# Talking-heads attention feeding a rational feed-forward layer: q padded to 128 columns, x, k and v moved in spaced pieces with a second v buffer, and the first tile's scores spread over three pairs of banks and two queues

## The chip, the cores and the metric

One core of a Trainium2 chip. A core has TensorE (PE, with its weight loads shown apart as PEld), VectorE (DVE), ScalarE (ACT), GpSimd (POOL) and SyncE (SP), which here does nothing but issue DMAs. The metric is the device time of one execution in microseconds, as the median of several runs; lower is better.

## The reference

Shapes: batch 4, 12 heads, 448 rows, head dimension 64; the feed-forward layer goes from 768 to 2048 and back over 1792 tokens.

```python
scores = scale * np.matmul(q, k.transpose(0, 1, 3, 2))
scores = np.einsum('bhij,hg->bgij', scores, w_pre)       # heads mixed before the softmax
attn = np.exp(scores - scores.max(-1, keepdims=True))
attn = attn / (attn.sum(-1, keepdims=True) + 1e-09)
attn = np.einsum('bhij,hg->bgij', attn, w_post)          # and after it
x = np.matmul(attn, v)                                   # -> (1792, 768)
h = x @ w_in
P = a0 + a1*h + a2*h**2 + a3*h**3
Q = 1 + abs(b0)*abs(h) + abs(b1)*h**2
out = (P / (Q + 1e-06)) @ w_out
```

## The kernel before, in words

The attention half works in 16 tiles T of query rows, four to a batch b: three of 120 rows and a short one of 88 (T = 0, 7, 11 and 15), held as 9 blocks of 10 rows. For each pair of heads `put_qk` (L428) multiplies q by k: one head in the lower 64 partitions, the other in the upper, each in two pieces of columns, `for i0, i1 in ((0, 64), (64, n))` (L435), with n = 120 or 90. The two results stand in two PSUM banks, taken from the pool `ps_s` of two. DVE or ACT copies each to a tile `st`, and SP issues a DMA, the shuffle (d<-st, L452), that lays the rows of ten blocks and twelve heads beside each other as D, so that one matmul can mix the heads. D has two buffers; a tile of twelve heads needs 13 shuffles, as the last head takes two.

`put_pre` (L488) takes two row blocks at a time, a step: it mixes the heads (PE, L504), takes the row maximum (DVE, L511), the exponential (ACT, L520) and the scale of each row. A tile has six steps, a short one five. The first step of a tile waits for all 13 shuffles of the tile. `put_post` (L562) mixes the heads again two steps later (PE, L569), and `put_av` (L607) multiplies by v twice for each tile (L618), two and three steps into the tile that follows. ACT casts that result into `xs` (L627), which holds x of one batch in one buffer; DVE writes the remainder (L631), and when the last tile of a batch is done, SP stores xs in two halves (L634), each of 1344 KB. v has one buffer and is loaded in four parts (L597), k two buffers (b > 0 in two parts, L351), q three (L339). Beside all this 36 of the 64 pieces of the feed-forward weights are loaded (cr, L367), turned from 64-bit into a pair of numbers by ACT, POOL and DVE, and stored (w_scr, L406); the other 28 follow in the second half.

The second half has 64 units. Each multiplies x by a part of w_in (PE, L762), goes through the rational function on ACT and DVE (its reciprocal, L796, is the longest), and multiplies by w_out (L836).

The order of every engine's work is set by a planner (`Plan.run`): each operation is added with engine, duration, dependencies, a due time `at` and sometimes an earliest time `since`. The planner walks through time on its own durations, takes for each free engine the ready operation with the earliest due time, and the program is written out in that order. Due times come from `tau`, which counts SLOT microseconds a step. The engines then run that order with semaphores, so a DMA that waits on SP holds back every DMA behind it.

Of the kernel before, what the change touches and what calls it, by code (L numbers as in the profile page):

```python
# [235 lines left out]
def mixed_attention_then_rational_ffn(ctx: ExitStack, tc, q, k, v, w, wmix, mask, a, b2, out):  # L236
# [25 lines left out]
    open_pools(base, "left", (("cr", 3), ("cm", 2), ("cg", 1), ("co", 2), ("xs", 1), ("xo", 2)))  # L262
    open_pools(left, "left", (("d", 1), ("e", 6), ("a", 2), ("v", 1)))
# [20 lines left out]
    SLOT, HALF = 4.4, 2.5  # L284
# [51 lines left out]
    def put_q(T, at):  # L336
        def load():
            Q[T] = sb["q"].tile([128, H // 2, TI], F32, tag="q", name="q")
            nc.sync.dma_start(out=Q[T], in_=q[T])  # L339

        q_ld[T] = add("sp", 0.63, load, [R["q"].take()], at=at, extra=dma(128 * H // 2 * TI * 4))

    def put_k(b, parts, at):
# [11 lines left out]
        for i in range(parts):  # L355
            k_ld[b].append(add("sp", 0.63, load(i), [free] + k_ld[b][:1], at=at + 0.8 * i, extra=dma(128 * n * S * 4)))
# [4 lines left out]
    def put_w(f, c, at):  # L361
# [57 lines left out]
        o8 = add("sp", 0.45, store, [o7], at=at, extra=dma(128 * CV * 8))  # L419
# [8 lines left out]
    def put_qk(T, pr, at):  # L428
# [17 lines left out]

        def shuffle(h, i0, i1):
            def fn():
# [3 lines left out]
                nc.sync.dma_start(  # L452
# [3 lines left out]
        slots = [R["ps_s"].take(), R["ps_s"].take()]  # L456
        o = pe(0.82, mm, [q_ld[T], k_ld[b][pr * len(k_ld[b]) // (H // 2)]] + slots, at=at, extra=0.16, mode="quarters")
        qk_op[T, pr] = o
        for hh in range(2):
# [4 lines left out]
            for i0, i1 in ((0, G10),) if h < H - 1 else ((0, G10 - 1), (G10 - 1, G10)):
# [5 lines left out]
                s_ = add("sp", 0.79, shuffle(h, i0, i1), [x for x in deps if x], at=at, extra=0.06 * (i1 - i0) * n / TI, after=after)  # L470
# [121 lines left out]
    def put_v(b, at):  # L592
# [14 lines left out]
    def put_av(T, hv, at):  # L607
# [365 lines left out]
```

## Time and profile before

| what | value |
|---|---|
| median of 3 runs | 1002.48 us (997.08 to 1003.05) |
| the profiled execution | 1004.43 us |
| its span | 1002.7 us |
| mean granted TensorE clock | 0.967 |
| busy share: PE, DVE, ACT, POOL | 92%, 78%, 46%, 28% |
| DMA | 173.58 MB, mean 173 GB/s |
| first step of tile 0 / first unit of the second half | 27.18 us / 523.02 us |

The span runs from the first to the last instruction of the profiled execution. PEclk is the share of TensorE's full clock, 2.4 GHz, that was granted. A row such as `[11.25 <-DMA d<-st]` says that the engine stood idle for 11.25 us before it and that the landing of a shuffle ended the wait. DMA share is the mean busy share of the core's 16 DMA engines.

### The profile page before, as it was taken

To read this page: it belongs to the slowest core of one execution; us is meant where nothing else is said; L and a number is where in the kernel's file an instruction comes from. 1 tells how busy PE (TensorE), PEld (TensorE's weight loads), DVE (VectorE), ACT (ScalarE), POOL (GpSimd) and SP (SyncE) were. 2 spreads that over 40 slices of the span, in tenths; PEclk is the share of its full clock that TensorE was granted. 3 is DMA by queue.
4 is the path that set the end of the run, shared out by engine and by line. 5 is a ranking of instruction groups with operands and counts; after the bars stand their busy time and mean duration, and the time that the engine had idled before them with its cause. 6 is when DMAs were issued, how large, how long until landed. Compare 5 with 4: busy or idle time off the path is not lost.

```text
span 1002.7 us, 17820 instructions
## 1 busy us (share of the span) xinstructions
PE 923.0 (92%) x6768; PEld 726.3 (72%) x6768; DVE 784.7 (78%) x1198; ACT 461.9 (46%) x1066; POOL 281.1 (28%) x288
## 2 busy tenths in 40 slices
PE   5878998699996999789989999999999999999996
PEld 1345666456564656555678999889899999999995
DVE  3657777587685886656758899999998889898995
ACT  2456566356564656534545355555533323333230
POOL 2222332233323333200242454555211111111110
PEclk9789999799998999989989999999999999999999
DMA  6864757655676556832569474643456141330212
GB/s 209 231 196 149 241 171 249 216 176 183 197 258 216 168 167 189 273 116 90 216 220 417 187 255 126 221 166 111 150 196 248 52 163 58 147 111 1 72 39 74
DMA packets 67561, 173.58 MB, mean 173 GB/s; under 512 B 6452, under 2 KB 47508, under 8 KB 63764
## 3 DMA queue, kind: packets, MB, share of 16 engines
q1 hardware_dynamic: 67476, 172.45, 51.3%
q8 instruction: 53, 0.87, 0.4%
q14 instruction: 32, 0.26, 0.1%
HBM read 86.53 MB, written 47.19 MB: 133 GB/s over the span
## 4 chain that ended last, share of the span: by engine, by line
PE 59%; DVE 17%; DMA 12%; issue 4%; ACT 4%; SPq 2%; POOL 2%; POOLq 0%; ACTq 0%; DVEq 0%
PE ps_s L762 15%; PE ps_a L569 10%; PE ps_t L836 7%; PE ps_s L438 7%; PE ps_t L504 6%; DVE rc L796 6%; PE ps_v L618 6%; DMA d<-st 5%; PE ps_a L836 5%; DMA cr<-in_w 4%; PE ps_v L836 2%; DVE cg L386 2%; DVE sq L793 1%; DVE cm L392 1%; SPq L452 1%
## 5 line engine op out<-in xcount | busy, mean ns | idle before, releaser
L569 PEld LDWEIGHTS ps_a<-krs,e 128*112 128x112 f32 x1440 | 157.2, 180 | 68.9 <-DVE nm L511 19.4
L796 DVE RECIPROCAL rc<-sq 128x448 f32<-128x448 f32 x64 | 188.4, 2943 | 0.9
L569 PE MATMUL ps_a<-krs,e 128*112 128x120 f32 x1440 | 174.4, 275 | 0.0
L809 POOL TENSOR_TENSOR g<-rc,g 128x448 fp32r<-128x448 f32 x60 | 71.7, 1195 | 297.4 <-DVE g L232 203.2
L504 PE MATMUL ps_t<-d,kpre 64*64 64x448 f32 x720 | 102.8, 588 | 51.0 <-DMA d<-st 35.1
L438 PE MATMUL ps_s<-kk,q 64*64 64x448 f32 (+2 forms) x768 | 132.9, 584 | 13.6 <-DMA kk<-in_k 6.2
L836 PE MATMUL ps_t<-g,w 128*128 128x448 f32 x576 | 142.6, 366 | 2.3 <-ACT o L875 1.4
L520 ACT ACTIVATE e<-ps_t,nm 128x448 f32<-128x448 f32 x180 | 112.5, 630 | 65.3 <-DVE nm L511 54.2
L511 DVE TENSOR_REDUCE nm<-ps_t 128x1 f32<-128x448 f32 x180 | 104.8, 615 | 48.2 <-PE ps_t L504 47.4
L773 ACT ACTIVATE m<-ps_s,a_sb 128x448 f32<-128x448 f32 x64 | 46.3, 724 | 191.3 <-PE ps_s L762 191.2
L377 POOL TENSOR_SCALAR cm<-cm 128x384 f32<-128x384 f32 x64 | 99.6, 1560 | 84.8 <-ACT cm L372 84.6
L762 PE MATMUL ps_s<-xs,w 128*128 128x448 f32 x576 | 122.4, 366 | 0.6 <-DVE m L789 0.6
L762 PE MATMUL ps_s<-x,w 128*128 128x448 f32 x576 | 121.8, 365 | 0.0
L836 PEld LDWEIGHTS ps_t<-g,w 128*128 128x128 f32 x576 | 107.9, 188 | 12.1 <-ACT o L875 2.2
L762 PEld LDWEIGHTS ps_s<-xs,w 128*128 128x128 f32 x576 | 108.4, 189 | 9.9 <-DVE m L789 1.4
L762 PEld LDWEIGHTS ps_s<-x,w 128*128 128x128 f32 x576 | 108.2, 188 | 8.3
L527 POOL TENSOR_SCALAR sm<-sm 128x2 f32<-128x2 f32 (+1 forms) x92 | 35.9, 390 | 249.1 <-ACT e L520 246.8
L232 DVE COPY aa<-ps_a 112x480 f32<-112x480 f32 x137 | 87.9, 653 | 22.3 <-PE ps_a L569 21.0
L836 PE MATMUL ps_a<-g,w 128*128 128x448 f32 x384 | 98.2, 365 | 0.0
L438 PEld LDWEIGHTS ps_s<-kk,q 64*64 64x64 f32 (+2 forms) x768 | 37.5, 133 | 82.6 <-issue 54.6
L232 DVE COPY st<-ps_s 120x448 f32<-120x448 f32 (+1 forms) x123 | 73.5, 616 | 25.2 <-PE ps_s L438 25.0
L403 POOL TENSOR_TENSOR co<-cm,co 128x384 fp32r<-128x384 f32 x64 | 69.3, 1083 | 76.5 <-ACT co L230 76.3
(47 smaller groups left out, 1104.9 us busy)
## 6 DMA issues: line engine op xcount, KB each, us to landing
d<-st SPq DMA_DIRECT2D x132, 210.0 KB
cr<-in_w SPq DMA_DIRECT2D x64, 384.0 KB
w_scr<-co SPq DMA_DIRECT2D x64, 384.0 KB
w<-w_scr SPq DMA_DIRECT2D x16, 1536.0 KB
x_scr<-xs SPq DMA_DIRECT2D x8, 1344.0 KB
x<-x_scr SPq DMA_DIRECT2D x3, 2688.0 KB
d<-st SPq DMA_DIRECT2D x44, 157.5 KB
q<-in_q SPq DMA_DIRECT2D x16, 360.0 KB
```

The source lines that it names most:

```text
L232: eng.tensor_copy(o, i)
L377: nc.gpsimd.tensor_scalar(out=m, in0=m, scalar1=F64_MIN, scalar2=F64_MAX, op0=ALU.max, op1=ALU.min)
L403: eng.tensor_sub(t[:, 1, :], box["m"].bitcast(F32), t[:, 0, :].bitcast(F32))
L438: nc.tensor.matmul(box["s"][hh][i0:i1, 0:S], lhsT=Q[T][d, pr, i0:i1], rhs=K[b][d, pr, :], start=True, stop=True)
L504: nc.tensor.matmul(box[r if nt == 2 else 0]["t"][64 * c:64 * c + 64, 0:S], lhsT=kpre[p], rhs=Dt[T][p, kb + c if nt == 2 else kb, :], start ...
L511: nc.vector.tensor_reduce(out=nm, in_=box[r]["t"][:, 0:S], axis=AX.X, op=ALU.max, negate=True)
L520: nc.scalar.activation(e, box[r]["t"][:, 0:S], AF.Exp, bias=box[r]["nm"], accum_out=box[0]["sm"][:, r:r + 1])
L569: nc.tensor.matmul(t[0:JT, j * P:(j + 1) * P], lhsT=box["e"][:, j * JT:(j + 1) * JT], rhs=box["kr"], start=True, stop=True)
L762: nc.tensor.matmul(h[:, 0:S], lhsT=W[fi][:, wi, kk * 128:(kk + 1) * 128], rhs=x[:, kk // 3, xj, kk % 3, :], start=(n == 0), stop=(n == 3 * ...
L796: nc.vector.reciprocal(new("rc"), box["vv"])
L809: eng.tensor_sub(g[:, 1, :], box["rc"], g[:, 0, :].bitcast(F32))
L836: nc.tensor.matmul(O[key][:, 0:S], lhsT=W[fi][:, wi, DM + m * 128:DM + (m + 1) * 128], rhs=box["g"][:, gi, :], start=(f == 0 and n == 0), ...
```

## The change

- q is padded from 120 to 128 columns, and the second piece of every pair of heads covers columns 64 to 128. The rows past n are not copied on.
- x of a batch is stored in 12 pieces of 224 KB instead of 2 of 1344 KB, the pieces 1.6 us apart in the plan, the first 5 us after the last value product.
- k of batches 1 to 3 is loaded in 6 pieces 7 us apart instead of 2 that are 0.8 us apart, from 40 us earlier. v has a second buffer, and its four parts are 8 us apart. To make room the output buffers `xo` open only in the second half.
- Tile 0's scores take their two banks in turn from `ps_s`, `ps_t` and `ps_a`, which are idle then, and the shuffles of its odd heads are issued by ACT instead of SP.
- In the plan, stores of w and x count as ready 2 us later than their data (`late`), their issue is costed a little differently, and SLOT is 4.2 instead of 4.4.

```diff
-            t = max([t, op.since] + [d.start for d in op.behind])
+            t = max([t + op.late, op.since] + [d.start for d in op.behind])
...
-    open_pools(base, "left", (("cr", 3), ("cm", 2), ("cg", 1), ("co", 2), ("xs", 1), ("xo", 2)))
-    open_pools(left, "left", (("d", 1), ("e", 6), ("a", 2), ("v", 1)))
+    open_pools(base, "left", (("cr", 3), ("cm", 2), ("cg", 1), ("co", 2), ("xs", 1)))
+    open_pools(left, "left", (("d", 1), ("e", 6), ("a", 2), ("v", 2)))
...
-    SLOT, HALF = 4.4, 2.5
+    SLOT, HALF = 4.2, 2.5
...
-            Q[T] = sb["q"].tile([128, H // 2, TI], F32, tag="q", name="q")
+            Q[T] = sb["q"].tile([128, H // 2, TQ], F32, tag="q", name="q")
...
-            k_ld[b].append(add("sp", 0.63, load(i), [free] + k_ld[b][:1], at=at + 0.8 * i, extra=dma(128 * n * S * 4)))
+            k_ld[b].append(add("sp", 0.45, load(i), [free] + k_ld[b][:1], at=at + gap * i, extra=dma(128 * n * S * 4), since=at + gap * i - 4.0))
...
-        o8 = add("sp", 0.45, store, [o7], at=at, extra=dma(128 * CV * 8))
+        o8 = add("sp", 0.57, store, [o7], at=at, extra=dma(128 * CV * 8), late=2.0)
...
-            box["s"] = [bank("s"), bank("s")]
-            for i0, i1 in ((0, 64), (64, n)):
+            box["s"] = [bank(ps_), bank(ps_)]
+            for i0, i1 in ((0, 64), (64, TQ)):
...
+        def other(h):
+            return T == 0 and h % 2 == 1
...
-                nc.sync.dma_start(
+                (nc.scalar if other(h) else nc.sync).dma_start(
...
-            v_ld[b].append(add("sp", 0.63, load(j), [free] + v_ld[b][:1], at=at, extra=dma(JT * H * D * 4), since=at))
+            v_ld[b].append(add("sp", 0.63, load(j), [free] + v_ld[b][:1], at=at + 8.0 * j, extra=dma(JT * H * D * 4), since=at + 8.0 * j))
...
-        def store():
-            nc.sync.dma_start(out=x_scr[b][:, hv], in_=Xs[b][:, hv].bitcast(F32))
+        def store(hl, p):
+            def fn():
+                nc.sync.dma_start(out=x_scr[b][:, hv, hl, p], in_=Xs[b][:, hv, hl, p].bitcast(F32))
+            return fn
...
-            o = add("sp", 0.63, store, x_done[b, hv], at=at, extra=dma(128 * 6 * S * 4))
+            for i in range(6):
+                o = add("sp", 0.45, store(i // 3, i % 3), x_done[b, hv], at=at + 5.0 + 1.6 * (2 * i + hv),
+                        extra=dma(128 * S * 4), late=2.0, since=at + 4.0 + 1.6 * (2 * i + hv))
...
-        put_k(b, 2, at=tau[first[4 * b - 2]])
+        put_k(b, 6, at=tau[first[4 * b - 2]] - 40.0, gap=7.0)
...
-        put_v(b, at=tau[first[4 * b] + LAG + 2] - 6.0 if b else 10.0)
+        put_v(b, at=tau[first[4 * b]] - 24.0 if b else 10.0)
...
-        put_qk(0, pr, at=-8.0 + pr)
+        put_qk(0, pr, at=-8.0 + pr, ps_="sta"[pr % 3])
```

TensorE's matmuls stand in the same order before and after, with other shapes and, for tile 0, other banks. What the planner moves is on SP and in which of ACT and DVE does a copy.

SP's queue before, in the step of tile 4 in which batch 0's x is done, up to tile 5's last head (x_scr0 is the store of batch 0, vv the load of batch 1's v, d_114 the D that tile 5 will read):

```order
L634 DMA x_scr0_137<-xs_692 128x2688
L452 DMA d_114<-st_1823 10x12x448
L452 DMA d_114<-st_1830 10x12x448
L406 DMA w_scr2_123<-co_1805 256x1x384
L597 DMA vv_1889<-in_v 112x768
L367 DMA cr_1900<-in_w 128x768
L634 DMA x_scr0_137<-xs_692 128x2688
L597 DMA vv_1889<-in_v 112x768 x3
L452 DMA d_114<-st_1907 10x12x448
L452 DMA d_114<-st_1919 9x12x448
```

After, around the same shuffles of tile 5 (d_111 is the same D):

```order
L457 DMA d_111<-st_1827 10x12x448
L457 DMA d_111<-st_1840 10x12x448
L640 DMA x_scr0_134<-xs_686 128x448 x2
L408 DMA w_scr2_120<-co_1817 256x1x384
L640 DMA x_scr0_134<-xs_686 128x448
L353 DMA kk_1647<-in_k 128x448
L369 DMA cr_1897<-in_w 128x768
L341 DMA q_1914<-in_q 128x768
L457 DMA d_111<-st_1916 10x12x448
L457 DMA d_111<-st_1923 9x12x448
```

The two whole stores and the four loads of v have left this place; three pieces of x, one of k and tile 7's q stand there now.

SP's queue before, three steps into the shuffles of tile 6 (d_113), with nothing of batch 0's x left:

```order
L452 DMA d_113<-st_2034 10x12x448
L367 DMA cr_2059<-in_w 128x768
L452 DMA d_113<-st_2070 10x12x448
L452 DMA d_113<-st_2084 10x12x448
L452 DMA d_113<-st_2131 10x12x448
L452 DMA d_113<-st_2135 10x12x448
```

After, at the same shuffles (d_110):

```order
L457 DMA d_110<-st_2034 10x12x448
L640 DMA x_scr0_134<-xs_686 128x448 x3
L353 DMA kk_1647<-in_k 128x448
L457 DMA d_110<-st_2073 10x12x448
L457 DMA d_110<-st_2083 10x12x448
L369 DMA cr_2106<-in_w 128x768
L640 DMA x_scr0_134<-xs_686 128x448
L369 DMA cr_2135<-in_w 128x768
L457 DMA d_110<-st_2139 10x12x448
L457 DMA d_110<-st_2137 10x12x448
```

The last four pieces of x of batch 0 now stand before and behind tile 6's shuffles of its third pair of heads. An ACT cast into the one xs buffer, later in tile 5, waits for them.

TensorE's first rows before, two pairs of heads of tile 0 and the first rows of the third (26 is the second piece of 90 rows):

```order
L438 MATMUL ps_s_162<-kk_151,q_149 64x448
L438 MATMUL ps_s_163<-kk_151,q_149 64x448
L438 MATMUL ps_s_162<-kk_151,q_149 26x448
L438 MATMUL ps_s_163<-kk_151,q_149 26x448
L438 MATMUL ps_s_176<-kk_151,q_149 64x448
L438 MATMUL ps_s_177<-kk_151,q_149 64x448
L438 MATMUL ps_s_176<-kk_151,q_149 26x448
L438 MATMUL ps_s_177<-kk_151,q_149 26x448
L438 MATMUL ps_s_192<-kk_151,q_149 64x448
L438 MATMUL ps_s_193<-kk_151,q_149 64x448
```

After:

```order
L440 MATMUL ps_s_159<-kk_148,q_146 64x448
L440 MATMUL ps_s_160<-kk_148,q_146 64x448
L440 MATMUL ps_s_159<-kk_148,q_146 64x448
L440 MATMUL ps_s_160<-kk_148,q_146 64x448
L440 MATMUL ps_t_166<-kk_148,q_146 64x448
L440 MATMUL ps_t_167<-kk_148,q_146 64x448
L440 MATMUL ps_t_166<-kk_148,q_146 64x448
L440 MATMUL ps_t_167<-kk_148,q_146 64x448
L440 MATMUL ps_a_189<-kk_148,q_146 64x448
...
L440 MATMUL ps_s_195<-kk_148,q_146 64x448
L440 MATMUL ps_s_196<-kk_148,q_146 64x448
```

The second pair takes two banks of ps_t and the third two of ps_a, and the fourth is the first to come back to ps_s; every piece has 64 columns.

ACT's first rows before:

```order
L230 COPY st_172<-ps_s_163 90x448
L331 ACTIVATE b1_sb_119<-b_sb_118 128x1
L230 COPY st_188<-ps_s_177 90x448
L230 COPY st_201<-ps_s_193 90x448
L230 COPY st_213<-ps_s_205 90x448
```

After:

```order
L232 COPY st_175<-ps_s_160 90x448
L457 DMA d_110<-st_175 10x9x448
L333 ACTIVATE b1_sb_116<-b_sb_115 128x1
L457 DMA d_110<-st_184 10x9x448
L232 COPY st_203<-ps_a_190 90x448
L457 DMA d_110<-st_203 10x9x448
L232 COPY st_225<-ps_t_205 90x448
```

ACT now copies and issues in turn; the rows with DMA are the shuffles of tile 0's odd heads.

## Rows read from the trace of the kernel before

**Rows 1.** The windows view: start and end of a stretch in us, its length, then busy time and number of instructions of PE, PEld, DVE, ACT and POOL, the granted clock, DMA share and GB/s. The stretches that begin at 27.18, 146.18, 184.15, 273.56, 308.81, 369.40 and 393.76 us are the whole tiles 0, 4, 5, 8, 9, 11 and 12, from the first step of the tile to that of the next; the last two are the start and the rest of the second half.

```profile
27.18:56.59 29.41, 20.55 (x132) 10.03 (x133) 16.21 (x35) 13.53 (x36) 8.47 (x10) 0.79 0.88 243
146.18:184.15 37.97, 26.72 (x289) 18.77 (x289) 24.44 (x52) 18.57 (x51) 10.62 (x14) 0.89 0.74 243
170.00:180.00 10.00, 2.90 (x27) 1.85 (x19) 5.49 (x14) 3.42 (x9) 2.91 (x4) 0.79 0.96 324
184.00:190.00 6.00, 5.85 (x31) 3.76 (x32) 2.31 (x4) 1.90 (x5) 0.23 (x1) 0.55 0.55 205
184.15:214.97 30.82, 30.01 (x289) 20.16 (x289) 24.02 (x49) 16.38 (x44) 9.96 (x11) 0.91 0.57 184
273.56:308.81 35.25, 26.45 (x282) 16.78 (x281) 24.64 (x56) 17.31 (x48) 9.61 (x13) 0.95 0.77 251
308.81:337.54 28.73, 28.73 (x288) 19.04 (x288) 22.44 (x44) 17.40 (x47) 10.59 (x11) 0.94 0.61 194
369.40:393.76 24.36, 24.07 (x261) 16.53 (x261) 14.73 (x34) 15.20 (x39) 7.50 (x9) 1.00 0.71 222
393.76:430.16 36.40, 25.91 (x282) 16.78 (x281) 24.35 (x56) 17.40 (x48) 8.08 (x12) 0.93 0.72 234
523.02:541.07 18.05, 17.40 (x81) 15.48 (x82) 13.77 (x17) 9.35 (x17) 3.04 (x4) 0.97 1.00 401
541.07:1002.60 461.53, 451.30 (x2224) 417.19 (x2222) 413.53 (x443) 183.66 (x333) 129.98 (x103) 1.00 0.39 138
```

**Rows 2.** The chain that ended last, in order of time, around tiles 5, 6, 9, 11 and 13: start us, length us, what. x8 and x16 are one step's pre-mix, one pair of heads' scores, one step's post-mix; x48 is one of a tile's two value products.

```profile
190.30 0.91 PE ps_t L504 x8
...
191.21 0.75 PE ps_s L438 x8
...
191.97 1.82 PE ps_a L569 x16
...
197.28 2.61 PE ps_v L618 x48
...
224.72 1.60 PE ps_s L438 x8
...
314.10 0.91 PE ps_t L504 x8
...
405.41 2.01 PE ps_v L618 x48
...
433.54 2.65 PE ps_a L569 x16
```

**Rows 3.** The timeline of PE at the first step of tiles 0, 1, 3, 4, 5, 9 and 13: start us, length us, then the instruction and in brackets the idle time before it with what ended it.

```profile
27.18 1.84 PE L504 MATMUL ps_t<-d,kpre 64*64 64x448 f32 x8 [3.41 <-DMA d<-st]
...
56.59 1.89 PE L504 MATMUL ps_t<-d,kpre 64*64 64x448 f32 x8 [6.45 <-DMA d<-st]
...
116.76 1.10 PE L504 MATMUL ps_t<-d,kpre 64*64 64x448 f32 x8 [2.50 <-DMA cr<-in_w]
...
146.18 1.10 PE L504 MATMUL ps_t<-d,kpre 64*64 64x448 f32 x8 [1.24 <-DMA d<-st]
...
184.15 1.89 PE L504 MATMUL ps_t<-d,kpre 64*64 64x448 f32 x8 [11.25 <-DMA d<-st]
...
308.81 1.89 PE L504 MATMUL ps_t<-d,kpre 64*64 64x448 f32 x8 [8.27 <-DMA w_scr<-co]
...
430.16 1.89 PE L504 MATMUL ps_t<-d,kpre 64*64 64x448 f32 x8 [10.26 <-DMA d<-st]
```

**Rows 4.** The timeline of SP's queue from 144 to 179 us: start us, length us, and the DMAs issued.

```profile
144.26 9.53 SPq L452 DMA_DIRECT2D d<-st  x6
...
162.73 0.35 SPq L634 DMA_DIRECT2D x_scr<-xs  x1
...
167.09 1.36 SPq L597 DMA_DIRECT2D vv<-in_v  x1
...
169.53 0.41 SPq L634 DMA_DIRECT2D x_scr<-xs  x1
...
169.99 3.22 SPq L597 DMA_DIRECT2D vv<-in_v  x3
...
173.31 5.36 SPq L452 DMA_DIRECT2D d<-st  x5
```

**Rows 5.** Groups of instructions, shapes kept apart: PEld's loads of q for the scores, by columns: busy us, mean ns of one | idle us before them.

```profile
L438 PEld LDWEIGHTS ps_s<-kk,q 64*56 64x56 f32 x288 | 19.6, 135 | 0.3 <-issue 0.3
...
L438 PEld LDWEIGHTS ps_s<-kk,q 64*26 64x26 f32 x96 | 3.2, 101 | 17.6 <-issue 17.6
```

**Rows 6.** The chain that ended last, in its first 30 us: start us, length us, what.

```profile
4.48 7.55 DMA kk<-in_k
...
24.47 2.67 DMA d<-st
```

**Rows 7.** The timeline of all engines in the first 30 us.

```profile
11.77 9.60 SPq L452 DMA_DIRECT2D d<-st  x8
...
14.65 1.88 PE L438 MATMUL ps_s<-kk,q 64*64 64x448 f32 x8 [0.65 <-ACT st L230]
...
22.80 0.98 PE L438 MATMUL ps_s<-kk,q 64*64 64x448 f32 x8 [0.71 <-DVE st L232]
```

**Rows 8.** The timeline of ACT at the first cast of batch 1's x.

```profile
199.93 0.46 ACT L230 CAST xs<-ps_v 128x360 fp32r<-128x360 f32 x1 [1.06 <-PE ps_v L618]
```

More of the change, by code (lines that the diff above doesn't have):

```diff
@@ L26 @@
 TI = 120
+TQ = 128
 NT = 4 * B
@@ L39, with __init__ @@
 class Op:
-    __slots__ = ("eng", "dur", "fn", "deps", "at", "extra", "start", "end", "left", "behind", "since", "n", "on", "pick", "mode")
-    def __init__(self, eng, dur, fn, deps, at, extra, since, mode):
+    __slots__ = ("eng", "dur", "fn", "deps", "at", "extra", "start", "end", "left", "behind", "since", "n", "on", "pick", "mode", "late")
+    def __init__(self, eng, dur, fn, deps, at, extra, since, mode, late):
+        self.late = late
         self.since, self.on, self.pick, self.mode = since, None, isinstance(eng, dict), mode
@@ L59, in __init__, with add @@
         self.ops = []
-    def add(self, eng, dur, fn, deps=(), at=0.0, extra=0.0, since=0.0, after=(), mode=None):
-        op = Op(eng, dur, fn, [d for d in deps if d is not None], at, extra, since, mode)
+    def add(self, eng, dur, fn, deps=(), at=0.0, extra=0.0, since=0.0, after=(), mode=None, late=0.0):
+        op = Op(eng, dur, fn, [d for d in deps if d is not None], at, extra, since, mode, late)
         op.behind = list(after)
@@ L337, in load, with put_k @@
         def load():
-            Q[T] = sb["q"].tile([128, H // 2, TI], F32, tag="q", name="q")
+            Q[T] = sb["q"].tile([128, H // 2, TQ], F32, tag="q", name="q")
             nc.sync.dma_start(out=Q[T], in_=q[T])
-        q_ld[T] = add("sp", 0.63, load, [R["q"].take()], at=at, extra=dma(128 * H // 2 * TI * 4))
-    def put_k(b, parts, at):
+        q_ld[T] = add("sp", 0.63, load, [R["q"].take()], at=at, extra=dma(128 * H // 2 * TQ * 4))
+    def put_k(b, parts, at, gap=0.8):
         free = R["k"].take()
@@ L451, in fn @@
                 p0 = place(i0, h)
-                nc.sync.dma_start(
+                (nc.scalar if other(h) else nc.sync).dma_start(
                     out=Dt[T][p0:p0 + STRIDE * (i1 - i0 - 1) + 1:STRIDE, 0:m, :], in_=box[h % 2][i0 * m:i1 * m])
             return fn
-        slots = [R["ps_s"].take(), R["ps_s"].take()]
+        slots = [R["ps_" + ps_].take() for _ in range(2)]
         o = pe(0.82, mm, [q_ld[T], k_ld[b][pr * len(k_ld[b]) // (H // 2)]] + slots, at=at, extra=0.16, mode="quarters")
@@ L469, in put_qk @@
                     after.append(shuf[T][0])
-                s_ = add("sp", 0.79, shuffle(h, i0, i1), [x for x in deps if x], at=at, extra=0.06 * (i1 - i0) * n / TI, after=after)
+                s_ = add("act" if other(h) else "sp", 0.79, shuffle(h, i0, i1), [x for x in deps if x], at=at, extra=0.06 * (i1 - i0) * n / TI, after=after)
                 st_use.append(s_)
@@ L706, in rest @@
         left.close()
-        open_pools(after, "left", (("wl", CH - NR), ("x", 1), ("t", 2), ("g", 3)))
+        open_pools(after, "left", (("wl", CH - NR), ("x", 1), ("t", 2), ("g", 3), ("xo", 2)))
     op_begin = add("sp", 0.0, begin, [on_right], at=-100.0)
@@ L952 @@
     given = {
-        "q": qt.reshape(4 * B, 128, H // 2, TI),
+        "q": qt.reshape(4 * B, 128, H // 2, TQ),
         "k": kt,
```

12 lines of the change are left out of this document (6 added, 6 removed).

## The prediction, made before the changed kernel ran

> **What bounds the kernel now.** I read the page's table of engines first, then the 40 slices, the chain that ended last, the windows cut at the tile starts, TensorE's timeline and SP's. TensorE is busy 92% of the span, and from 541 us on there is nothing to gain from this change: 451.30 of 461.53 us busy at clock 1.00 [rows 1]. The change leaves TensorE's order the same there, so I carry that half over unchanged. What is loose is the attention half, before 523 us.
>
> Its floor comes from three groups of matmuls per step of two row blocks: 0.91 (pre-mix, L504) + 0.75 (one pair of heads' scores for the next tile, L438) + 1.82 (post-mix, L569) = 3.48 us, and two value products of 2.61 us a tile [rows 2]. A tile of six steps should take 6 x 3.48 + 2 x 2.61 = 26.1 us, one that runs beside a short tile's products, of 2.01 us each, 24.9 [rows 2]. The windows cut at the tile starts say 29 to 38 us [rows 1]. Three things fill the gap.
>
> First, waits at the start of a tile, where every shuffle (d<-st) of the tile must have landed: 11.25 us at tile 5, 8.27 at tile 9, 10.26 at tile 13, and 6.45, 2.50 and 1.24 at tiles 1, 3 and 4 [rows 3]. The three long ones are one place in each batch: the whole of x (two stores of 1344 KB) and of the next v (four loads of 336 KB) is issued between 162.73 and 173.2 us, ahead of the tile's last shuffles [rows 4]. From 170 to 180 us the DMA engines are then 0.96 busy at 324 GB/s and TensorE works 2.90 us in 10 [rows 1].
>
> Second, the clock. After such a wait TensorE runs at the lower of its two levels, 1.2 GHz: from 184 to 190 us the granted clock is 0.55 [rows 1]. The step from 184.15 to 190.30 us takes 6.15 us instead of 3.48, those from 308.81 to 314.10 and from 430.16 to 436.19 (the end of 433.54 + 2.65) 5.29 and 6.03 [rows 2, 3]. That is 2.7 + 1.8 + 2.5 = 7.0 us.
>
> Third, in tiles 6, 10 and 14 the scores of the next, short tile take 1.60 us a pair instead of 0.75 [rows 2]. A short tile has 90 rows, taken as 64 + 26 columns; the weight loads of 26 columns have 17.6 us of idle time before them, those of 56 columns 0.3 [rows 5].
>
> **The change, part by part.** All sums are against the profiled execution, 1004.43 us (span 1002.7), which lies 1.95 us above the median of the three runs.
>
> *q at 128 columns.* Every pair becomes 64 + 64. The pair of 64 + 56 takes 0.75 us and two full halves of the pre-mix 0.91, so I take 0.75 and have 0.91 as the other end. Three short tiles have 18 such pairs on a full TensorE: 18 x 0.85 = 15.3 us (12.4 by the other end). Not all of it stays: in the long tiles the shuffles had 5 us more to land. I give back 0.6 us a tile and take 13.5; with the 12.4 and a wait like tile 4's 1.24 [rows 3] at each it would be 8.7, and I use 8. The added bytes, 24 KB in each of 16 loads, are 0.4 MB, 1.2 us of DMA over the whole half at 325 GB/s (243 at a share of 0.74 is 328, [rows 1]): hidden, as the queues are.
>
> *x in pieces, k in six, v spaced into a second buffer.* Counted from SP's order, what stands between tile 4's last shuffle and tile 5's is 13 shuffles (2.58 MB), six w pieces in or out and x and v: 8.68 MB before, 7.51 after; for tile 6 6.07 before, 7.18 after. The later batches: tile 9 9.46 to 7.30, tile 10 6.07 to 7.21, tile 13 9.07 to 6.61. So the lump is split in two, not removed. At the 243 GB/s that tile 4's window averaged, waits included [rows 1], 7.51, 7.30 and 6.61 MB need 30.9, 30.0 and 27.2 us, where 37.97, 35.25 and 36.40 were used [rows 1]: 21.5 us saved, and the tiles behind them need 29.5 and 29.7 against 30.82 and 28.73: 0.3 more. That is 22 us. At the 325 GB/s of a full share they fit under the floor, and all of 29.8 + 7.0 = 36.8 us goes. At the 222 GB/s of the best undisturbed tile [rows 1] it is 33.8, 32.9 and 29.8, 13.1 saved, and 5.3 lost again behind them: 8. I take 24, near the middle row. x in rows of 1.8 KB instead of 10.8 costs something: the w loads' long rows reach 401 GB/s at a share of 1.00 [rows 1], so 2.75 MB go from 6.9 us to 8.5, 1.6 us of DMA time per batch, inside those bounds. The 14 more issues per batch take SP some 0.4 us each, as the stores do now [rows 4]; SP has room, as its thirteen shuffles of 0.8 us and the rest fill some 17 of 26 us.
>
> *First tile.* Now each pair waits for the two banks of the pair before: at 14.65 us 0.65 of idle time and 1.88 of matmul, 2.5 us a pair [rows 7]. With three pairs of banks that goes, but the second third of k lands at 12.03 us (4.48 + 7.55) whatever else is done [rows 6]. From there four pairs at the 0.98 us of 22.80, or the 1.88 of 14.65 [rows 7], end at 16 to 19.5 instead of 22.1, and thirteen shuffles of 0.8 us on one queue (SP's row of 11.77 has eight in 9.60 us [rows 7]) become seven and seven on two. ACT gives up some 0.8 us for each of its issues and has nothing else to do there. So tile 0 can start 3 to 6 us before 27.18. But from 27 to 57 us the DMA engines are 0.88 busy [rows 1], and about the same bytes stand ahead of tile 1 (11.7 MB before, 11.9 after): I take 3 us, from -1 to 6.
>
> *The planner's numbers* (store 2 us later, k 40 us earlier, SLOT 4.2) move k and w issues from in front of shuffles. The waits at tiles 1, 3 and 4, 10.2 us together [rows 3], can shrink or grow by that; I take 2.5, from -5 to 9.
>
> *The added wait.* x has one buffer. Its last piece now stands behind tile 6's sixth shuffle, and the ACT cast that opens the next batch's x waits for it; before, both stores were issued 30 us ahead of that cast (162.73 and 169.53 against 199.93 [rows 4, 8]). 4.6 MB stand from tile 5's last shuffle to the last piece: 14 us at 325 GB/s, 19 at 243, and the cast comes 15.8 us after the tile's start. Behind it in ACT's queue are the exponentials and score copies. I count 0 to 3 us a batch; it is inside the 24.
>
> Sum: 13.5 + 24 + 3 + 2.5 = 43; 1004.4 - 43 = 961.4, and 1.95 less for the median: 959.5, so 960.
>
> **Rivals.** *DMA stays at 222 GB/s.* The pieces spread the load, but thirteen shuffles a tile queue behind whatever is there, and no undisturbed tile moved more [rows 1]. Then 8 instead of 24, and q's gain is 8, as TensorE waits in tiles 6 and 10: 1002.5 - 8 - 8 - 3 - 2.5 = 981. For it: tile 5's and 6's loads are both above 7 MB. Against: the disturbed tiles averaged 234 to 251 with idle time in them [rows 1].
>
> *The long waits don't come from x and v.* If the late shuffles were held by SP's own order (a w store waiting for POOL ahead of them), spacing x gives nothing: 1002.5 - 13.5 = 989, or 992.5 and up with q's lower end. Against: DMA 0.96 busy from 170 to 180 [rows 1].
>
> *All borders clear.* 15.3 + 36.8 + 6 + 9 = 67: 935. It needs DMA at full share whenever a tile asks for it.
>
> *Slower: the single x buffer.* If ACT's cast stands waiting, TensorE stops with it, three times. To end above 1002.5 it must eat the 43 us, 14 us a batch; at 18 us a batch the time is 1002.5 - 43 + 54 = 1013. The last piece would then have to land 18 us after the cast is ready, so 4.6 MB would take some 34 us, 136 GB/s, less than any tile with such a load shows. That is what speaks against it.
>
> *Slower: each piece pays its own latency.* The last shuffle of tile 0 took 2.67 us from issue to landing [rows 6]. Fourteen more DMAs a batch, if each waited for the one before, would be 37 us a batch, 112 in all: 1002.5 - 43 + 112 = 1072; it decides from half of that on. Against it, the row of 144.26 has six shuffles issued in 9.53 us [rows 4], where one after the other would need 16. The Trainium skill speaks against this change too (DMA: Bandwidth & Descriptors, section Bandwidth): transfers should be batched to 1 MiB or more to get three quarters of the peak rate. By its table, an estimate of 200 GB/s for pieces of 0.23 MB makes a batch's 4.1 MB of x and k 20 us instead of 12, some 25 us in all. The trace does not agree where many are in flight: from 369 to 394 us, with no x and no v, only pieces of 0.2 to 0.4 MB and smaller, 222 GB/s at a share of 0.71 is 313 at a full one [rows 1].
>
> **How the numbers follow.** A measurement of this kernel can tell about 1% from no change. Forecast (945 to 973) 0.60; DMA at 222 (973 to 985) 0.16; borders clear (under 945) 0.11; spacing gives nothing 0.07, half of it inside 1%; slower by the x buffer 0.04, by latency 0.02. Faster by over 1%: 0.60 + 0.16 + 0.11 + 0.03 = 0.90; within 1%: 0.05; slower: 0.05. The range for 8 in 10 goes to 933 and 984.
>
> **What would show it.** L438 in tiles 6, 10 and 14 at 0.75 to 0.91 us a pair, and no 26-column form. The waits of 8 to 11 us at tiles 5, 9 and 13 cut to 3 us or less, with tiles 4, 8 and 12 at 28 to 31 us and tiles 5 and 9 unchanged near 30; DMA share there 0.75 to 0.85 and never a 10 us stretch at 0.96. Tile 0 at 22 to 25 us. No ACT idle time over 3 us before the first xs cast of a batch. From the first feed-forward unit on, the same 480 us. Wrong would be: waits of the old length at those tiles, or new ones two steps into tiles 5, 9 and 13 with ACT waiting for a DMA.

## The result and the profile after

The changed kernel takes 968.52 us (median of 4 runs, 967.71 to 974.27) against 1002.76 us of before on the same chip: 34 us less; the ratio of the means is 0.9682 (95% interval 0.963 to 0.9734), which is 32 us. Ratios here and below go by the means of the executions, and they leave out one of 960.38 us in the last experiment, which lies 2% above the fastest of its kernel. The profiled execution took 967.71 us, its span is 965.9 us and its mean granted clock 0.983 (before 0.967). 960 was forecast, 933 to 984 the range.

Cut where the first unit of the second half starts, the two executions compare thus: the attention half ends at 480.40 us instead of 522.95, 42.5 us earlier, and the second half takes 485.53 us instead of 479.70, 5.8 us longer. The windows of the changed kernel answer to [rows 1]: columns as there; the stretches are tile 0, tile 4, ten microseconds in which about a third of batch 0's x is issued, tiles 5, 8, 9, 12 and 14, and then the whole of either half.

```profile
28.14:53.22 25.08, 20.12 (x132) 10.22 (x133) 14.44 (x32) 12.17 (x33) 4.60 (x8) 0.84 0.77 212
140.29:170.48 30.19, 27.36 (x288) 18.92 (x289) 23.73 (x51) 17.42 (x49) 10.84 (x13) 1.00 0.77 244
160.00:170.00 10.00, 8.19 (x88) 5.42 (x84) 7.53 (x15) 5.80 (x17) 2.87 (x4) 1.00 0.94 314
170.48:199.52 29.04, 27.23 (x288) 18.84 (x289) 22.60 (x48) 16.77 (x46) 8.78 (x11) 1.00 0.81 259
251.71:283.78 32.07, 28.95 (x282) 17.50 (x281) 24.59 (x54) 17.36 (x48) 10.10 (x13) 0.95 0.72 229
283.78:311.82 28.04, 27.33 (x289) 19.01 (x289) 23.50 (x49) 17.68 (x48) 9.81 (x12) 1.00 0.76 232
365.32:396.60 31.28, 26.34 (x282) 16.85 (x281) 23.61 (x53) 17.78 (x49) 9.56 (x14) 1.00 0.66 214
424.54:450.69 26.15, 25.59 (x281) 18.36 (x281) 19.84 (x42) 14.11 (x40) 1.23 (x6) 1.00 0.28 80
...
28.14:480.40 452.26, 420.10 (x4408) 286.76 (x4409) 340.21 (x724) 260.87 (x706) 136.90 (x171) 0.98 0.67 211
480.40:965.93 485.53, 469.64 (x2306) 431.59 (x2304) 430.54 (x458) 194.81 (x353) 141.22 (x111) 1.00 0.42 149
```

Tiles 4, 8 and 12 fell from 37.97, 35.25 and 36.40 us to 30.19, 32.07 and 31.28, and tiles 5 and 9 didn't pay for it (30.82 and 28.73 before). The DMA engines are 0.94 busy at 314 GB/s from 160 to 170 us, about as in the lump of before (0.96 at 324), but TensorE now works 8.19 us of those 10 and not 2.90. The load is about the same; what changed is that a tile's last shuffles no longer stand behind the whole lump. Tile 14 took 26.15 us, the floor of 26.1 that the prediction worked out.

TensorE's first steps of tiles 5, 9 and 13, as in [rows 3]: the waits of 11.25, 8.27 and 10.26 us are 2.29, 0.30 and 3.52, and over tiles 5 and 9 the clock stays at 1.00.

```profile
170.48 1.10 PE L509 MATMUL ps_t<-d,kpre 64*64 64x448 f32 x8 [2.29 <-DMA d<-st]
...
283.78 1.13 PE L509 MATMUL ps_t<-d,kpre 64*64 64x448 f32 x8 [0.30 <-DMA x_scr<-xs]
...
396.60 1.10 PE L509 MATMUL ps_t<-d,kpre 64*64 64x448 f32 x8 [3.52 <-DMA x_scr<-xs]
```

The name behind an arrow is inferred. This step reads the shuffled scores, not x: at tile 13 SP issued the tile's last shuffle at 391.92 us, behind six pieces of x and one of w, and by the trace's records that shuffle lands at 396.50 us.

The loads of q, answering to [rows 5]: one form of 64 columns is left. The rows after it are pairs of heads' scores for the next, short tile, in the chain at tiles 6, 10 and 14: 0.75 us as in the long tiles of [rows 2], where before had 1.60. These three tiles are 27.96, 29.02 and 26.15 us long, for 31.69, 31.85 and 30.14.

```profile
L440 PEld LDWEIGHTS ps_s<-kk,q 64*64 64x64 f32 x736 | 35.9, 139 | 50.1 <-issue 34.9 <-ACT st L232 7.7 <-DVE st L234 4.7
```

```profile
200.64 0.75 PE ps_s L440 x8
...
312.92 0.75 PE ps_s L440 x8
...
425.64 0.75 PE ps_s L440 x8
```

SP's queue at the place of [rows 4]: x goes out one to three pieces at a time, with shuffles between.

```profile
166.63 1.14 SPq L640 DMA_DIRECT2D x_scr<-xs  x1
...
169.20 1.69 SPq L457 DMA_DIRECT2D d<-st  x2
170.95 2.06 SPq L640 DMA_DIRECT2D x_scr<-xs  x3
...
173.78 1.65 SPq L457 DMA_DIRECT2D d<-st  x2
```

And ACT at the first cast of batch 1's x, as in [rows 8]: it does not wait for x's last piece. But the step in front of it, on a weight piece, stood 4.76 us for the landing of that piece, with the cast, score copies and exponentials behind it.

```profile
186.62 0.55 ACT L374 ACTIVATE cm<-cr 128x384 f32<-128x384 f32 x1 [4.76 <-DMA cr<-in_w]
187.31 0.46 ACT L232 CAST xs<-ps_v 128x360 fp32r<-128x360 f32 x1
```

Waits of this kind are together the largest of ACT's in the attention half of after. The group of that step, first of before, then of after, each from 27 to 523 us (42 pieces); what stands behind the second bar is ACT's idle time in front of it. Of after this takes in the first 43 us of the second half, but the 55.4 us all lie before it:

```profile
L372 ACT ACTIVATE cm<-cr 128x384 f32<-128x384 f32 x42 | 23.4, 556 | 47.8 <-DMA cr<-in_w 46.1 <-POOL co L403 1.7
```

```profile
L374 ACT ACTIVATE cm<-cr 128x384 f32<-128x384 f32 x42 | 23.5, 564 | 56.9 <-DMA cr<-in_w 55.4 <-POOL sm L532 1.1 <-POOL co L405 0.2
```

What TensorE waits for in that half after the change, in us, times, and longest (the 9.9 is the start of tile 0), and then its wait for exponentials before the change:

```profile
PE ps_t L509 <- DMA kk<-in_k: 12.8, 2, 9.9
PE ps_t L509 <- ACT e L525: 7.7, 6, 2.8
PE ps_t L509 <- DMA d<-st: 5.7, 5, 2.3
```

```profile
PE ps_t L504 <- ACT e L520: 2.1, 4, 0.8
```

All landings together fell from 45.9 us, without the start of tile 0, to 25.0 with it; the exponentials that come late from ACT rose from 2.1 to 7.7.

### The profile page after: what moved, and what is told of

The parts are those of the page before. It is cut to its first block, busy times and chain, and to the rows that moved or that the text cites. A ratio compares the mean times of both kernels' runs of the same rounds, so it can differ in the third digit from the quotient of the medians.

```text
span 965.9 us, 17871 instructions
## 1 busy us (share of the span) xinstructions
PE 898.4 (93%) x6768; PEld 721.1 (75%) x6768; DVE 781.6 (81%) x1194; ACT 460.3 (48%) x1067; POOL 285.0 (30%) x291
## 4 chain that ended last, share of the span: by engine, by line
PE 49%; DVE 18%; DMA 15%; issue 6%; ACT 5%; POOL 4%; SPq 2%; POOLq 0%; ACTq 0%; DVEq 0%
PE ps_s L771 16%; PE ps_t L845 8%; PE ps_a L574 7%; DMA cr<-in_w 6%; DMA d<-st 5%; PE ps_a L845 5%; PE ps_t L509 5%; DVE rc L805 5%; PE ps_v L623 3%; PE ps_s L440 3%; PE ps_v L845 3%; POOL cm L379 2%; DVE nm L516 2%; DVE cm L394 2%; ACT e L525 2%
## 5 line engine op out<-in xcount | busy, mean ns | idle before, releaser
L818 POOL TENSOR_TENSOR g<-rc,g 128x448 fp32r<-128x448 f32 x63 | 75.1, 1192 | 306.7 <-DVE g L234 205.3
L509 PE MATMUL ps_t<-d,kpre 64*64 64x448 f32 x720 | 105.8, 575 | 33.6 <-DMA kk<-in_k 12.8
L379 POOL TENSOR_SCALAR cm<-cm 128x384 f32<-128x384 f32 x64 | 96.9, 1518 | 93.8 <-ACT cm L374 93.6
L440 PE MATMUL ps_s<-kk,q 64*64 64x448 f32 x736 | 107.5, 571 | 7.5 <-DMA kk<-in_k 5.3
L234 DVE COPY aa<-ps_a 112x480 f32<-112x480 f32 x144 | 91.5, 651 | 11.8 <-PE ps_a L574 9.6
L405 POOL TENSOR_TENSOR co<-cm,co 128x384 fp32r<-128x384 f32 x64 | 71.6, 1121 | 56.8 <-ACT co L232 56.7
L623 PE MATMUL ps_v<-aa,vv 112*64 112x120 f32 (+1 forms) x1536 | 81.0, 262 | 6.1 <-DVE xs L636 5.5
L623 PEld LDWEIGHTS ps_v<-aa,vv 112*64 112x64 f32 x1536 | 74.1, 137 | 10.2 <-DVE xs L636 6.0
```

The lines of the kernel that those rows point to most:

```text
L234: eng.tensor_copy(o, i)
L379: nc.gpsimd.tensor_scalar(out=m, in0=m, scalar1=F64_MIN, scalar2=F64_MAX, op0=ALU.max, op1=ALU.min)
L440: nc.tensor.matmul(box["s"][hh][i0:i1, 0:S], lhsT=Q[T][d, pr, i0:i1], rhs=K[b][d, pr, :], start=True, stop=True)
L509: nc.tensor.matmul(box[r if nt == 2 else 0]["t"][64 * c:64 * c + 64, 0:S], lhsT=kpre[p], rhs=Dt[T][p, kb + c if nt == 2 else kb, :], start ...
L623: nc.tensor.matmul(t[64 * hf:64 * hf + 64, pr * n:(pr + 1) * n], lhsT=V[b][:, j, g, :], rhs=A[T][:, j, g, 0:n], start=(j == 0), stop=(j == ...
L818: eng.tensor_sub(g[:, 1, :], box["rc"], g[:, 0, :].bitcast(F32))
```

## The experiments

Times are medians against runs of the kernel before on the same chip (1002.6 to 1004.1 us). A difference of two ratios is given with the root of the sum of their half intervals squared, in us of a 1002 us kernel. "After" is the changed kernel. Every edit makes the planner write another order for SP, ACT, DVE and POOL, so a difference holds the edit's own effect and some of the order's.

**One part of the change undone.** q back at 120 columns (`TQ = 120`, pieces `(0, 64), (64, n)`):

> The changed kernel with q at 120 columns again, second piece up to n (26 columns in the short tiles). If the padding is worth what the first sum took, 13.5 us, the time is 982 us against 968.5, and tiles 6, 10 and 14 take 31 us again instead of 28, 29 and 26. If those tiles are held by their DMA load instead (7.2 MB for the tile behind tiles 5 and 9), it is 974 us or less, the narrow pairs being back at 1.60 us while the waits at the next tile's start shrink by as much.

Measured: 976.52 us, ratio 0.9729 (0.9667 to 0.979), 5 us over after, give or take 8. Tiles 6, 10 and 14 are 31.38, 33.32 and 30.93 us again, 12.4 together over after's 27.96, 29.02 and 26.15, yet other tiles are shorter than after's. What the padding is worth by itself this run leaves open.

x in two stores, k in two loads and one v buffer, all as before:

```diff
-            for i in range(6):
-                o = add("sp", 0.45, store(i // 3, i % 3), x_done[b, hv], ...)
+            o = add("sp", 0.63, whole, x_done[b, hv], at=at, ...)
-        put_k(b, 6, at=tau[first[4 * b - 2]] - 40.0, gap=7.0)
+        put_k(b, 2, at=tau[first[4 * b - 2]])
-        put_v(b, at=tau[first[4 * b]] - 24.0 if b else 10.0)
+        put_v(b, at=tau[first[4 * b] + LAG + 2] - 6.0 if b else 10.0)
```

> The changed kernel with x stored in two halves, k in two parts and v in four parts into one buffer, with the due times of the kernel before. If the lumps of x and v make the long waits, the waits of 8 to 11 us at tiles 5, 9 and 13 are back and the time is 990 to 995 us. If the long waits come from SP's order (a store of weights that waits ahead of the shuffles), the waits stay at 2 to 4 us and the time within 5 us of 968.5.

Measured: 994.52 us, ratio 0.9897 (0.9837 to 0.9956): 22 us over after, give or take 8. TensorE's first steps of tiles 5, 9 and 13 show the long waits again, with the clock at its lower level behind them (1.89 to 1.95 us for eight matmuls, 1.10 in the rows of after above):

```profile
181.44 1.89 PE L509 MATMUL ps_t<-d,kpre 64*64 64x448 f32 x8 [9.55 <-DMA w_scr<-co]
...
308.66 1.89 PE L509 MATMUL ps_t<-d,kpre 64*64 64x448 f32 x8 [9.39 <-DMA cr<-in_w]
...
423.95 1.95 PE L509 MATMUL ps_t<-d,kpre 64*64 64x448 f32 x8 [7.64 <-DMA d<-st]
```

So the lumps make the long waits, and not a store of weights that holds up SP's queue. But not all of the loss lies there: tiles 4, 8 and 12 take 37.66, 33.91 and 32.29 us, 10.3 more than in after, and tile 0 starts 4.4 us later, at 32.52 us. The rest is spread over other tiles.

Only the two whole stores of x, with k and v spaced as in after:

> The changed kernel with only x stored in two halves again; k and v stay spaced. Putting x, k and v back together cost 22 us (994.5 against some 972 on that chip). If x, two thirds of the lump, makes the long waits, tiles 4, 8 and 12 take 34 us or more each and the time is 983 or above. If x and v only hurt together, the tiles stay near 31 us and the time is 975 or less.

Measured: 975.64 us, ratio 0.9722 (0.9666 to 0.9777), 4 us over after, give or take 8; tile 4 is 33.04 us, not 37.66 as in the run above. The waits at tiles 5, 9 and 13 are 4.58, 6.02 and 4.76 us, between those of after and those of the whole lump, and the clock falls behind them:

```profile
172.10 2.00 PE L509 MATMUL ps_t<-d,kpre 64*64 64x448 f32 x8 [4.58 <-DMA d<-st]
...
289.77 1.89 PE L509 MATMUL ps_t<-d,kpre 64*64 64x448 f32 x8 [6.02 <-DMA d<-st]
```

So a whole x brings some 9 of 20 us of these waits back, though the time shows only 4, give or take 8. Lumping k and v as well costs 18 more, give or take 8. Which of k, v and v's second buffer makes these 18 was not taken apart.

The first tile's scores in `ps_s` alone, all shuffles on SP:

> The changed kernel with tile 0's scores in two banks and all its shuffles on SP, as before. Tile 0 did not start earlier with the change (28.1 us against 27.2), but tile 1 did, by 3.4 us. If that is the first tile's edits, tile 1 starts at 56 to 57 us again and the time is 972. If it comes from the lighter k, v and weight loads of that stage, tile 1 stays at 53 us and the time at 968.

Measured: 974.24 us, ratio 0.9699 (0.9654 to 0.9745): 2 us over after, give or take 7. Tile 0 starts at 26.22 us, earlier than after's 28.14, and tile 1 at 52.46 (53.22). The three pairs of banks and the second queue bring nothing that can be seen.

SLOT back at 4.4:

> The changed kernel with the planner's SLOT at 4.4 as before. The second half took 485.5 us instead of 479.7 from its first matmul on. If that is the due times (all of the second half's are 18 us earlier with 4.2, so the planner sets weight pieces ahead of the units on ACT and DVE), the second half is back at 480 us and the time is 963. If it is the moved output buffers or only another order by chance, the second half stays above 483 us.

Measured: 970.07 us, ratio 0.9658 (0.9611 to 0.9706), second half 484.28 us. SLOT costs and gives nothing that shows, and it is not what made the second half longer. Tile 5 took 37.43 us in this plan (29.04 in after), with one wait of 7.37 us for DVE in its middle, and other tiles made up for it.

**How much is the plan's chance.** One constant of the planner moved (`HOP = 0.13` for 0.12), so that the order changes a little everywhere:

> The changed kernel with the planner's cost of a hand-over between engines at 0.13 us instead of 0.12, which means nothing by itself but writes another order. It tells how far the time moves by the order's chance alone. If the differences of 3 to 6 us between single edits are chance, single tiles move by 2 us and more and the time by up to 5 us either way; if they are causes, the time is within 2 us of 968.5 and the second half at 485.

Measured: 973.92 us, ratio 0.9706 (0.9643 to 0.977), second half 482.32 us, single tiles up to 5.4 us from after's (tile 9, 33.45 against 28.04). By the ratios it is 2 us over after, give or take 8. Differences of a few us between two plans, or of some us in one tile, can't be put down to an edit.

**What is left on the path.** ACT's step on a weight piece 4 us later in its order, all else as in after:

```diff
-        o1 = add("act", act(CV), mag, [ld, R["cm"].take()], at=at)
+        o1 = add("act", act(CV), mag, [ld, R["cm"].take()], at=at, late=4.0)
```

> The changed kernel, with the ACT step that opens a weight piece planned 4 us later than its load, so that it stands later in ACT's queue. In the changed kernel ACT idles 55 us in the attention half ahead of that step, waiting for the load (25 times), with exponentials behind it. If that is what keeps the tiles 2 to 6 us above the 26.1 us floor, ACT's wait falls under 25 us, the tiles lose 1 us each and the time is about 955. If those waits are beside the path, the time stays within 4 us of 968.5.

Measured: 953.93 us, ratio 0.9507 (0.945 to 0.9564), 18 us under after, give or take 8; the changes of SLOT and HOP moved it by 2. ACT's idle time before the step is gone:

```profile
L374 ACT ACTIVATE cm<-cr 128x384 f32<-128x384 f32 x43 | 23.8, 559 | 0.3 <-DMA cr<-in_w 0.3
```

Tiles 8 and 12 come down to the floor, 11.6 us less together. Tile 4, the first of the rows below, doesn't: 31.63 us for 30.19. Between the two profiled executions the attention half is 10.7 us shorter, so nearly all of it lies in these two tiles and what the others gain and lose cancels.

```profile
136.06:167.69 31.63, 28.00 (x289) 19.29 (x289) 23.51 (x48) 17.80 (x48) 9.16 (x12) 0.93 0.74 238
251.32:277.31 25.99, 24.45 (x280) 16.85 (x281) 22.25 (x48) 17.21 (x47) 9.70 (x12) 1.00 0.81 268
360.87:386.60 25.73, 24.34 (x281) 16.45 (x281) 22.35 (x51) 18.28 (x50) 10.54 (x13) 1.00 0.74 241
```

The second half's weight pieces spread over 31 units of time instead of 26 (`END1 + 31 * UNIT * ...`):

> The changed kernel with the 28 weight pieces of the second half due over 31 units instead of 26. The second half takes 485.5 us where the floor of its matmuls is some 479. If its extra waits (on ACT's copies of o and on DVE and POOL for g) come from weight pieces crowding those engines, it falls to 481 us or less and the time to 964. If they come from the order at the turn of an x block alone, it stays at 484 or more.

Measured: 964.32 us, ratio 0.9619 (0.9573 to 0.9666), 6 us under after, give or take 7; its second half takes 481.10 us instead of 485.53. TensorE's longest waits there, first of before, then of after (this run has 2.0 and 1.4 for ACT's o and 0.3 for g):

```profile
PE ps_t L836 <- ACT o L875: 1.4, 2, 0.8
PE ps_t L836 <- POOL g L809: 0.9, 2, 0.6
```

```profile
PE ps_t L845 <- ACT o L884: 4.3, 4, 1.7
PE ps_t L845 <- POOL g L818: 1.1, 2, 0.8
PE ps_t L845 <- DVE g L234: 0.7, 1, 0.7
```

That the spreading does it is not shown: the run with a whole x and the one with the first tile's old scores have second halves of 481.30 and 481.53 us without it.

**One part alone, on the kernel before.** The padding:

> The kernel before with q at 128 columns and full second halves in the scores, nothing else. Theory of the prediction: the 18 pairs of tiles 6, 10 and 14 fall from 1.60 to 0.75 us, 15.3 us, of which 13.5 (8 at the least) reach the end: 989 (987 to 995). Rival, from the run that took the padding out of the changed kernel and cost only some 5 us: tiles 6, 10 and 14 gain 3 to 4 us each, but what they gain the next waits for a shuffle or a k piece give back, since the loads of x and v come in one lump here: 995 to 999, with tile 5 or 7 and the tiles behind longer than before.

Measured: 988.62 us, ratio 0.9856 (0.984 to 0.9873): 14.4 us, give or take 1.7, and the rival falls. Its tiles 6, 10 and 14 are 29.11, 28.61 and 26.06 us where before had 31.69, 31.85 and 30.14: 9.9 us, which the padding explains. Tile 4 is 2.5 us shorter as well (35.46), and that may be the order, which is nearly before's but not quite.

ACT's late step on the kernel before (with the planner's `late`, which before has not):

> The kernel before with one thing from outside the change: ACT's first step on a weight piece (cm<-cr) is placed 4 us later in its order, so that the piece's load has landed (the planner takes a delay for it as the changed kernel's does). In the changed kernel that took 17 us off. If ACT's wait for weight pieces (44.1 us in the attention half of before) was on the path there too: 985 to 992. Rival: before, the long waits for shuffles at tiles 5, 9 and 13 come from the lump of x and v and stay at 8 to 11 us, so that only the shorter tiles gain: 995 to 1000. ACT's idle time before that step falls under 2 us by either.

Measured: 985.56 us, ratio 0.9835 (0.9812 to 0.9857): 16.5 us, give or take 2.3. ACT's idle time in front of the step is 0.8 us instead of 47.8, so the wait was on the path before the change too, and by about the same price. The long waits at tiles 5, 9 and 13 stay, as the rival said (9.89, 8.53 and 8.25 us), but tiles 0 to 4, 8 and 12 are 1.5 to 3.6 us shorter each:

```profile
L373 ACT ACTIVATE cm<-cr 128x384 f32<-128x384 f32 x41 | 22.6, 562 | 0.8 <-DMA cr<-in_w 0.8
```

**Two edits together, on after.** `late=4.0` and the 31 units together:

> The changed kernel with ACT's step on a weight piece 4 us later and the second half's weight pieces spread over 31 units of time instead of 26. Each alone gave 954 and 964 against 968 to 972. If the two losses are apart (attention half 441 us, second half 481): 948 to 951. Rival: the order of the second half is a matter of chance and the spreading gave nothing by itself: 952 to 957 with a second half of 485 to 487.

Measured: 946.65 us (942.53 to 953.64), ratio 0.9451 (0.9401 to 0.9501), the fastest kernel here but for the next, which can't be told from it. Its halves are 440.82 us from tile 0 on (after 452.26) and 480.80 us (485.53), the 441 and 481 that were expected if the two losses are apart; the time is a little under the 948 to 951 of that sum. The first is ACT's step; for the second the spreading is again not told from the order's chance.

The same, with ACT's step on b out of the way of tile 0:

```diff
-    b1_op = add("act", 0.15, ..., [ab_ld], at=40.0)
+    b1_op = add("act", 0.15, ..., [ab_ld], at=40.0, since=60.0)
```

> The same as the run before it, and ACT's step on b (which waits until 10.9 us for b's landing, with the first shuffles and copies behind it) stands later in ACT's order. If that wait holds tile 0: its first step moves from 27 us to 23 to 25.5. Whether the end moves with it: theory now, from the run with the first tile's old scores, that tile 1's start goes by the k and weight loads of the first 50 us: the end within 2 us of the run before it. Rival (the prediction's 3 us): the end 2 to 4 us earlier, 945 to 948.

Measured: 946.39 us (942.0 to 960.38), ratio 0.9427 (0.9399 to 0.9454): 2 us under the run before it, give or take 6, which fits both readings. Whether b's wait holds tile 0 stays open, since the profiled execution is the one of 960.38 us.

## Why the prediction was right, and where it was not

The time came out 8.5 us over the forecast, inside the range and inside the likeliest case (945 to 973). The two large terms have their mechanism shown by runs. That the attention half came out at 42.5 us less, where the sum said 43, is closer than these terms are known, and partly luck: one term gave nothing, and a wait that the prediction didn't see kept two tiles long. By its steps:

- *The padding, taken at 13.5 us (8 to 15.3).* Right: 14.4 alone on the kernel before, 9.9 of them in the three tiles that were priced (12.4 there when it is taken out of after). Taken out of after it cost 5, give or take 8, less than it gave; the two intervals just touch, and whether the padding is worth less among the other edits is not settled. The row of 0.75 us a pair is as forecast.
- *x, k and v, taken at 24 us (8 to 36.8).* Right in total and in the cause: 22, give or take 8, when undone. From before to after tiles 4, 8 and 12 are 16.1 us shorter and the tiles behind them, 5, 9 and 13, another 4.0. The waits that were to shrink to 3 us or less are 2.29, 0.30 and 3.52, the last a little over. Tiles 4, 8 and 12 were to take 28 to 31 us and took 30.19, 32.07 and 31.28. The price itself, bytes over a rate, holds for tile 4 alone: tile 12 was to take 27.2 us at 243 GB/s and 29.8 at 222, and took 31.28 with the DMA engines 0.66 busy, so its length was not set by them (the last item says by what). The counts of bytes were partly off too: five w pieces, not six, stand in the 8.68 MB, and from SP's queue as it ran tile 9 gets 8.8 MB instead of 7.30, the others are within about 0.5 of what was counted. The stretch of 160 to 170 us still has the DMA engines at 0.94, which I had said would not come again; it did no harm there. The working priced one lump and did not say which of its parts made it: x alone brings about half of the waits back.
- *The first tile, taken at 3 us (-1 to 6).* The step failed: tile 0 was to start at 22 to 25 us and started at 28.14, against 27.18 before. Shown is that the old scores do no worse (26.22, and 2 us in all, inside the error). What was said of TensorE came true: the last pair of scores ends at 18.20 us, inside the 16 to 19.5, and the last shuffle of tile 0 has been issued by 21.9 us (25.2 before). What failed is the time from issue to landing. The chain of after's start has shuffles that take 6.4 to 7.0 us, against 2.67 for the last one in [rows 6]:

```profile
17.24 0.96 PE L440 MATMUL ps_s<-kk,q 64*64 64x448 f32 x8
```

```profile
11.01 6.98 DMA d<-st
...
18.77 6.43 DMA d<-st
```

  I had left each shuffle that 2.67 us, and it was the wrong row: it is the second piece of the last head, 15.8 KB where the others have 142 to 158, and it moved while the DMA engines were 0.44 busy (24.47 to 27.18 us). By the trace's records of landings the other shuffles of tile 0 in before took 3.0 to 7.1 us. In after the same small piece, issued at 21.04 us, lands 7.1 us later, with the engines 0.85 busy, just as the tile starts. Over ten microseconds the engines compare thus (windows of before, then of after; the last two columns are share and GB/s):

```profile
20.00:30.00 10.00, 5.88 (x32) 1.59 (x30) 2.17 (x4) 1.54 (x4) 0.00 (x0) 0.78 0.67 190
```

```profile
20.00:30.00 10.00, 1.86 (x12) 1.28 (x16) 1.54 (x3) 1.19 (x3) 1.49 (x1) 0.62 0.84 225
```

  On SP's queue a weight piece and a q, 384 KB each, now stand ahead of the tile's last shuffles (18.32 and 19.17 us); before, a v piece of 336 KB did. That the landings are late because of them fits these rows; no run with fewer bytes in the first 30 us was made. Tile 0 itself got shorter, 25.08 us for 29.41, with its DMA share down from 0.88 to 0.77; since the run with the old first tile has its tile 1 at 52.46 us too, that does not come from this edit, and loads that stand later fit it.
- *The planner's numbers, 2.5 us (-5 to 9).* Not told apart: SLOT alone does nothing, and one plan differs from the next by some us.
- *The second half, taken as unchanged.* This step failed, by 5.8 us: 485.53 for 479.70. I had argued from TensorE's order, which is indeed the same. But the order of ACT, DVE and POOL in that half is planned anew, with the weight pieces at other places. TensorE waits 4.3 us for ACT's output step and 1.8 for the numerators g, 3.8 more than the 1.4 and 0.9 of before; the rest of the 5.8 is not accounted for. SLOT is not the cause. Spreading the weight pieces gave 481.10 and 480.80, and the other kernels made from after 481 to 486, so how much of it is the order's chance stays open. The 5.8 us are most of what is missing from 43 (42.5 saved in the attention half, less 5.8; the profiled execution is 36.7 us shorter).
- *The added wait for the one x buffer, 0 to 3 us a batch.* It doesn't come: no wait for x stands before the cast at 187.31 us, nor before those of the other two batches. The rival built on it fell, as did the one of latency: after the change 314 GB/s flow in pieces of 0.4 MB and less.
- *What was not seen at all.* "Three things fill the gap" left out a fourth. ACT's idle time before its step on weight pieces, 46.1 us for DMA, stood in the list of groups, and I read it as idle time of an engine that is not the bottleneck. Removing it gave 16.5 us (give or take 2.3) on before and 18 (8) on after. Near the end of tile 8 of after it can be seen how it reaches TensorE. ACT's row first, then the chain of waits with TensorE's row at its end, then two windows of four microseconds, one behind this place and one behind the 3.52 us at tile 13:

```profile
273.28 0.56 ACT L374 ACTIVATE cm<-cr 128x384 f32<-128x384 f32 x1 [3.06 <-DMA cr<-in_w]
```

```profile
273.92 1.51 POOL cm L379
...
275.45 0.04 DVE cm L383
...
276.94 0.54 DVE nm L516
...
277.50 0.73 ACT e L525 x2
...
278.28 0.88 PE ps_t L509 x3
```

```profile
278.28 0.88 PE L509 MATMUL ps_t<-d,kpre 64*64 64x448 f32 x3 [2.80 <-ACT e L525]
```

```profile
278.00:282.00 4.00, 3.72 (x18) 1.39 (x19) 3.42 (x7) 2.05 (x8) 0.22 (x1) 0.57 0.74 239
...
398.00:402.00 4.00, 4.00 (x27) 3.13 (x24) 2.33 (x6) 1.77 (x5) 0.21 (x1) 0.58 0.68 233
```

  ACT waits 3.06 us for the piece; POOL's step on the same piece follows, then DVE's, and DVE's remainder of x and its row maximum (nm) stand behind that in its order. The exponential is late, TensorE idle for 2.80 us, and for the next four microseconds it runs at a granted clock of 0.57. Both kernels have it, so it explains little of the 8.5 us, but it is why tiles 8 and 12 stayed at 31 to 32 us, which the run without it brought to 26.

## What to carry to other kernels

Ask of a bulk transfer what stands behind it on the queue. Here the same load on the DMA engines (0.94 and 0.96 busy) left TensorE 8.19 or 2.90 us of work in ten, by where the small urgent shuffles stood. Take a landing time from a row with the same size and the same load: 2.67 us of a small piece at a share of 0.44 was no measure for shuffles at 0.84. An engine that is busy 46% of the span can still hold the path when one step in its order waits for a load; look at what stands behind that step, on the engines that follow it too, and place it where the load has landed. Where a planner writes the order, "unchanged" has to be checked on every engine, and a few us between two plans prove nothing.

## What was not expected of the hardware

After TensorE's waits of 2.29 and 2.69 us in the changed kernel (tiles 5 and 11) the granted clock stayed at 1.00. After the 2.80 us at 278.28 it was 0.57 for four microseconds. After the 3.52 us at tile 13 the first eight matmuls still took 1.10 us, and only from about 398 us on was the clock 0.58. So, by an estimate, each of these two waits cost some 1.7 us more (4 x 0.43), the second not at its end but a little later. The length of the wait alone does not tell: in the run with ACT's step 4 us later, TensorE waited only 1.91 us before tile 4, and the clock was 0.55 for the next two microseconds.

```profile
136.06 1.95 PE L509 MATMUL ps_t<-d,kpre 64*64 64x448 f32 x8 [1.91 <-DMA d<-st]
```

```profile
136.00:138.00 2.00, 1.94 (x12) 1.47 (x16) 0.00 (x0) 0.00 (x0) 0.44 (x1) 0.55 0.94 312
```
